# The same 2,542 operations of two linear and two windowed attention layers, issued after another table of orders, engines and PSUM banks

## The chip, the cores and the metric

The kernel runs on one NeuronCore of a Trainium2 chip. The core has five instruction queues that run beside one another and meet only at semaphores: TensorE (PE, the matrix engine, with its weight loads shown apart as PEld), ScalarE (ACT), VectorE (DVE), GpSimd (POOL) and SyncE (SP, which only issues DMAs here). The program gives each queue a written order. The metric is the device time of one execution in microseconds, less is better; the time before is 410.37 us, the median of three runs (410.02 to 410.41).

## The reference

The input is x, 2048 tokens by 512 features, in bf16. Four layers are added to it one after the other, A, B, A, B, with shared weights for the two A and for the two B:

```python
x = x + A(layernorm(x));  x = x + B(layernorm(x));  x = x + A(layernorm(x));  x = x + B(layernorm(x))
# A: linear attention, 32 heads of 16
pq, pk = phi(q), phi(k)                # phi(t) = (t + 1 if t > 0 else exp(t)) + 1e-6
kv = sum over tokens of pk^T v;  z = sum of pk
o = (pq @ kv) / (pq . z + 1e-6);  out = o @ wo
# B: attention in a causal window of 256 tokens, 32 heads of 16
p = softmax(q k^T / 4, masked);  out = (p @ v) @ wo
```

## The kernel before, in words

The 2048 tokens are 16 tiles of 128, numbered 0 to 15. A class `Plan` writes down every piece of work as an `Op` in a dependency graph; a `Kernel` replays it on the five queues. In what follows, an operation is called by its name in the plan and its tile.

The work comes in four stages that flow into one another. In the first (`layer_a_keys`), each tile is loaded into `xres` and normalised (`norm`): `stats`, `aggr` and `xn` on VectorE, `eps` on GpSimd or VectorE, `pow` on GpSimd. The normalised tile is then transposed (`transpose`, L377 and L383): tiles 0 to 4 by TensorE (`T`, then the copy `Te`), tiles 5 to 15 by a DMA that SP issues. After it follow the keys (`k`, two matmul groups, L406), the first half of the sum over tokens (`g`, L481, two groups for each tile) and the queries (`q`, two groups, L420). Keys and queries each pass through `E` (the exponential, ScalarE, L429), `E1` (VectorE, L430) and `phi` (VectorE, L431). When all 16 tiles are through, `z`, `ge`, `gv` (L495), `den`, `rec`, `spread`, `M` and `pqd` close the sum over all tokens. `fill` (L268) are ten matmuls on zeros whose result nobody reads; besides them TensorE runs nine such at its start (L984).

The second and the fourth stage (`middle`) are the B layers. For each tile: the output and residual of the A layer before (`aout`, `res`), `norm` and transpose, the projections `bq`, `bk`, `bv`, the DMAs `kd` and `vd` that SP issues to lay out keys and values, the scores `s` (L638, L677, L680), their exponentials `ex` (ScalarE, L648, L690), the masks `mk` (VectorE) and `mf` (GpSimd or VectorE, L708 and L709), the weighted sums `pv` (L729), `rcp`, `div`, the transpose `oT` and the output `bout` with its residual `res`. In the second stage the norm, keys and values of the next A layer (`k`, `v`) are worked in as tiles become ready; the third stage (`barrier(2)`) then closes that sum as before. In the last tile `b_last` splits the transpose in two halves (L764) and the output into three groups of matmuls (L775).

SP's queue begins with the loads of `setup`. Their names: `x0`, `x1`, `x2`, `x4`, `x6`, `x8`, `x12` are pieces of x (131 KB for each tile), `wAk`, `wAq`, `wAv`, `wAo`, `wBv`, `wBo` are 0.52 MB each and `wBn` is 1.05 MB. A load from `x8` on also waits for the landing of the load four places before it in this list: x0, wAk, x1, x2, wAq, x4, x6, x8, x12, wAv, wAo, wBn, wBv, wBo. So `wAo` waits for `x6`, `wBn` for `x8`, and `wBv` for `x12`.

What sets the order is not the code but `TABLE`, a compressed string of bytes. `place` unpacks it: first the place of each of the 2,542 operations in one list, then the engine of each, then the PSUM bank of each of the 1,007 tiles in PSUM. Each engine runs its operations in the order of that list. A tile that takes a bank waits for the users of the tile that had it. `place` adds one more rule, which stays as it is: a GpSimd operation that is not in `SHORT` waits for the last VectorE operation in the list before it whose name is in `WIDE` (`E1`, `xn`, `mk`, `mf`):

```python
if o.eng == "POOL" and o.name not in SHORT and wide and wide not in o.deps:
    o.deps.append(wide)
if o.eng == "DVE" and o.name in WIDE:
    wide = o
```

`synchronise` turns the dependencies into semaphore waits.

Of the kernel before, what the change touches and what calls it, by code (L numbers as in the profile page):

```python
# [11 lines left out]
P = 128  # L12
D = 512
DH = 16
S = 2048
T = 16
# [207 lines left out]
class Plan:  # L224
# [632 lines left out]


TABLE = (
    r"c-qZa1K1|VvaT*P*0yciwr$(CZQHhO+qTW@CcDXcb7%hV<eVfoo0F4!@AKUGhSk+o?^{*fGyMUCh3765goc+c9E6835CI|rLPAiG2oggihztY|-3#}`C",  # L860
    r"4r=n43a|>hzijl3kWoa6p#`avO+fK1uY;ujD@Ez2SkS$&>LDpE9e8oAQe1v8a6_D$N)JZ7i0tjaUd=@c<fq38+hjCLu%LreIXx=gZ!`=YC|392gRX3jE",
    r"8s-6Ba;xXbbJY!USjp?I9C9aCKn-420Zp80tY9=m1@zK6Hc3&>dnyIY<i)AUHIJK`<CP!bC^_O<)o%ghj9zmcUi$1Y4j7Y=t3k1dhTn*aop79W;b4Py#",
    r"x`WOxo!U?>cOGEf$#LQi-BFJUPxgXItmuE7^L4%guZOoQoA9lpZPumWzvN{Fjw!EBfV!=XHU2d|(4Y=<4N6L!H|m;p0kHSC5}a023~lW+<^DHU4HgD@(",
    r"-N}%?_Ew~MLpedY&Gw>S1syz@+B~;(TS-1;7z#BLZ;Z=H72~d$@RTG*)26YbZ!F?D3BViO&1yK*+Eo4-gR3epF{Rlrn1Qk(5QUz5ZRaj+KSyU3G)k84K",
    r"s>rH{DypKWf=~#mKvb1fy@O;bxpFGH8VzHhw#urqsbVU-%Aty@5~`$%rgEyvkW!^kxl}1tTIE({RaI3@l~Gkx0jQ($KwhY;>Zt~*vZ}6XsFtdgYOQLjT",
    r"B^QU18ZR&6ow*D6xyhUs;z3I8mo4yiE6K!tBTN6HB&9rde{Ip-~#M}{cr#}sDm(CjZq=s5j=*uYM!bFW7Rk{QjJm<VVxSU)~iEM5+<mLYQDMzlhgur85",
    r"XJ|s-xPVp1@O>tlq;1n4)H=nQE3=q&BL>YKfYvrm5+wlez+%)Mm9`9aRU^QuPcvt1fDeI;OU$t?Hm!sk*9<uu9c})vBB7u0FvswOj?m;J8A~R=3n~6#|",
    r"2);OdSl1t-)=bxQS6Au$wQRoB#QbzN;!C9ouZhSMs9I;;+<N9wUEh1*p~6-t%H&=>}HsGaJGx~ZaL42+4-)C<*9mBF&OOYK(A)jf4zmBTZtmkNt})LB&",
    r";o~m=|fm)+3sEg{nTB~AX0!)Mn@uez{XYirAq-tU<ysK`gI2aG(Vr@K&=WrCB#|wB7M`IEkgYj{nN`|RaYV}UNS0B_H^-;Z5KdPTpQcR8^AsnVr;V}Y^",
    r"#c?<uBVt;W0uy5etcaDcGVWE8FeRo_bulug!i*RN>){oZ2`{S&I1w9Q6|9Q&F*9bt)OZPF;bp9Y)$o&QhAnV5&cV6Z96zf`_(gqHKP$jS*ch{7Hq4GW@",  # L870
    r"Gf4#?^Hv)hxf4wHpN#;AtK>xH5q?UQ*bJ_!mHQ@b7E_}hS#y2`d;-`jOA5Zte`5YN-7Q3z+9LXJ7X8@iVH9uw#0>)8@pk5%z$|?FXlr*jZrZ_7QjUq4H",
    r"u(9i%YNv&PRvKuqRH#7-}h|$CxUX>V*YyIZnqJ7+b|rE3go*!mYRsx8n|6iG5UGRUOyhIxLL+)Bx2RS7U!w1jEr<T#rSu7>1_^R2(BxB#KP)@EJbG7kC",
    r"4A;x62cd+-N*gEz4<RiU?d3m@SVe29;+5B9~ExEG^PRLY~OQa_AFc~yTLfcaE@)ebx0U7CdhaS%Sm0_q;M$4)pHhv1JGpAt|)x=#buAoU%-#u?NRXJR#",
    r"~PBo||?Zf@}3OC?Jyn_dDCVj%sIEyyn_qYXXQ40EkUvW0gp`Q^bB`HEmMX4zX#iH1hjN;Hx9ENGAHXX#Il$?g+2poy&XfAEW=oEuuQhjPb4=@8A!ozq3",
    r"(^5{#MYpjbJ)lhVkXlkkBFas9s1+rmN0gqJgftz+%(Rl)QXLwsT2mWpPl@RmKBgzMidIuQ>Oeo?dwhrSs4mr`yp)gf(+4a-9jOU5rB2kD3X-9&)Sa5qa",
    r"Xf(^@g#Pm=G2eYQGc38mK+76`LuxI(kVQR184&Ur$RK4TF`nbOkHRb^`IgYf{Icx8bpI>Ej^_nw3&v|7Ro|dX)6_{5>%2F(jr<+*=PxEqwTbmcF;1~NF",
    r"gZ{4N)W1P?eoRQy3~mKhPT*uHMoxwTpIB4%$PBI58*Tq@0Y`P-!YdWhpF`qsCO8l5+~~NiV4vrQ~NcjC#{|G@M4zNE$_r=oRgw*R-Gd&~y5p4$~2OL8I",
    r"v?9is#EiN4Sp9z$bkFYTnYypEgmJNiuTX&il}7Tl5#Q7S%8<LLyQq!08n0r&M@8mH(qt>?^~g@2-~oSJ{6kJO4=a~md3!)aNVIRuB~P@IF?a!wA-nhz3",
    r"kE<QtN=^UM>c07S5QXUS&VR;fwrYV$;^Ko7d$KkmM=jIEvfs1i|UQX$`D6gOl{3HLw@3=h|;6i+nE>UsL#+RuqZ{$rJfy;4cF3%OXAQ$G%+?Ts>f9}9t",
# [189 lines left out]
```

## Time and profile before

| | |
|---|---|
| runs (median of three) | 410.37 us |
| profiled execution, first to last instruction | 408.2 us |
| what lies around the span (the median less the span) | 2.2 us |
| TensorE busy | 396.0 us, 97% |
| VectorE busy | 347.9 us, 85% |
| ScalarE busy | 344.4 us, 84% |
| GpSimd busy | 113.8 us, 28% |
| granted TensorE clock | 1.000 |

The profiled execution has no time of its own apart from its span; the 2.2 us is the part of a run that lies before the first and after the last instruction. "Busy" is the time in which at least one instruction of the engine was under way. A matmul's end is modelled and matmuls overlap, so that a busy TensorE may still wait now and then. A row of a timeline has the start, the length, the engine, the line, the operation, what is written and read, the shape, and how many instructions were merged; an idle time before it stands in brackets with what ended it. A "q" behind an engine's name is its issuing queue.

### The profile page before, as it was taken

The numbers are of one execution on the slowest core, as the hardware profiler recorded it, in microseconds if no ns is written. First come the engines' busy times: TensorE is split into PE (matmuls) and PEld (weight loads), VectorE is DVE, ScalarE is ACT, GpSimd is POOL, SyncE is SP. The second block draws the span as 40 slices with busy tenths as digits, with TensorE's granted clock in tenths as the row PEclk, the third lists the DMA queues.
The fourth block names the chain that finished last, engine by engine and source line by source line (L and its number), as shares of the span: only waits on it lengthen the run. The fifth ranks groups of instructions, "written<-read, shape, count | busy, mean of one in ns | idle before, by whom it ended". The sixth has DMA issues, their size and how long they took to land.

```text
span 408.2 us, 18082 instructions
## 1 busy us (share of the span) xinstructions
PE 396.0 (97%) x7997; PEld 263.4 (65%) x7997; DVE 347.9 (85%) x808; ACT 344.4 (84%) x443; POOL 113.8 (28%) x194
## 2 busy tenths in 40 slices
PE   8999999999999999999999999999999999999996
PEld 3654676666575566666666777676757766576664
DVE  5998799999998999888977789988898778876685
ACT  3655579999999999999998355999998999999992
POOL 3553632112253343330503202122123201302212
PEclk9999999999999999999999999999999999999999
DMA  8754014923242934344231100364225542442543
GB/s 247 243 118 104 2 42 121 184 56 97 65 119 52 132 73 108 75 104 106 62 69 36 29 2 28 89 127 78 71 76 130 143 83 61 66 121 62 118 109 104
DMA packets 67654, 37.88 MB, mean 93 GB/s; under 512 B 48248, under 2 KB 62712, under 8 KB 67576
## 3 DMA queue, kind: packets, MB, share of 16 engines
q1 hardware_dynamic: 67184, 35.67, 38.1%
q8 instruction: 63, 1.03, 1.1%
q0 software_dynamic: 384, 1.05, 0.8%
q14 instruction: 15, 0.12, 0.1%
q10 hardware_dynamic: 8, 0.00, 0.0%
HBM read 6.29 MB, written 2.10 MB: 21 GB/s over the span
## 4 chain that ended last, share of the span: by engine, by line
PE 81%; ACT 10%; DVE 7%; DMA 1%; issue 1%; DVEq 0%
PE ps L406 27%; PE ps L420 20%; PE ps L729 15%; PE ps L638 8%; ACT pb L648 7%; PE ps L680 2%; PE ps L481 2%; ACT pb L690 1%; DVE XQ L563 1%; PE ps L677 1%; DMA XQ<-vp 1%; PE ps L984 1%; PE ps L457 1%; PE ps L543 1%; PE ps L268 1%
## 5 line engine op out<-in xcount | busy, mean ns | idle before, releaser
L648 ACT ACTIVATE pb<-ps 128x1024 bf16<-128x1024 f32 (+3 forms) x224 | 198.2, 966 | 7.4 <-PE ps L638 6.2
L729 PEld LDWEIGHTS ps<-vB,pb 128*128 128x128 bf16 x2560 | 77.6, 96 | 11.5 <-issue 4.2
L729 PE MATMUL ps<-vB,pb 128*128 128x34 bf16 x2560 | 83.2, 177 | 0.3
L420 PE MATMUL ps<-xT,wBp 128*128 128x128 bf16 x1024 | 68.6, 219 | 0.1
L420 PEld LDWEIGHTS ps<-xT,wBp 128*128 128x128 bf16 x1024 | 58.4, 98 | 9.6 <-issue 4.0
L708 POOL TENSOR_SCALAR_AFFINE_SELECT pb<-pb 128x1024 bf16<-128x1024 bf16 x34 | 39.1, 1149 | 84.0 <-DVE pb L700 31.9
L429 ACT ACTIVATE tE<-ps 128x512 bf16<-128x512 f32 x64 | 38.1, 606 | 18.4 <-PE ps L406 12.1
L638 PE MATMUL ps<-XQ,kB 32*128 32x256 bf16 (+2 forms) x1024 | 48.7, 262 | 3.3 <-ACT pb L648 0.6
L574 DVE TENSOR_TENSOR xres<-ps,xres 128x512 bf16<-128x512 f32 x63 | 43.1, 685 | 9.6 <-PE ps L406 9.1
L690 ACT ACTIVATE pb<-ps 128x1024 bf16<-128x1024 f32 x50 | 49.0, 1048 | 1.3 <-PE ps L680 1.0
L406 PE MATMUL ps<-wA,XQ 128*128 128x512 bf16 x192 | 49.2, 380 | 0.7 <-DMA XQ<-vp 0.6
L369 POOL TENSOR_SCALAR ve<-mv 128x1 f32<-128x1 f32 x49 | 11.8, 240 | 127.9 <-DVE mv L368 126.9
L370 POOL TENSOR_TENSOR rs<-ve,negh 128x1 f32<-128x1 f32 x64 | 37.9, 592 | 32.0 <-DVE ve L369 27.5
L367 DVE BATCH_NORM_STATS2 stats<-xres 128x6 f32<-128x512 bf16 x64 | 43.8, 685 | 2.8 <-DMA xres<-in_A_x_dram 2.1
L638 PEld LDWEIGHTS ps<-XQ,kB 32*128 32x128 bf16 x1024 | 15.7, 92 | 31.4 <-ACT pb L648 8.3
L420 PE MATMUL ps<-XQ,wA 128*128 128x128 bf16 x512 | 34.4, 219 | 0.0
L406 PE MATMUL ps<-wBv,xT 128*128 128x512 bf16 x128 | 34.3, 380 | 0.0
L406 PE MATMUL ps<-M,XQ 128*128 128x512 bf16 x128 | 33.3, 380 | 0.2
L420 PEld LDWEIGHTS ps<-XQ,wA 128*128 128x128 bf16 x512 | 30.1, 98 | 5.1 <-issue 0.6
L406 PE MATMUL ps<-wBo,oT 128*128 128x512 bf16 x124 | 32.7, 380 | 0.6 <-DVE vp L431 0.4
L656 DVE TENSOR_TENSOR pb<-pb,tri 128x512 bf16<-128x512 bf16 x68 | 27.7, 419 | 3.7 <-ACT pb L648 3.1
L741 DVE TENSOR_TENSOR o<-ps,rc 128x256 bf16<-128x256 f32 x64 | 27.0, 422 | 1.7
(114 smaller groups left out, 545.9 us busy)
## 6 DMA issues: line engine op xcount, KB each, us to landing
vB<-vS SPq DMA_DIRECT2D x64, 136.0 KB, 2.6
kB<-vp SPq DMA_DIRECT2D x64, 128.0 KB, 2.2
wA<-in_A_wqkv_dram SPq DMA_DIRECT2D x3, 512.0 KB, 5.2
xres<-in_A_x_dram SPq DMA_DIRECT2D x2, 512.0 KB, 4.8
pb<-in_B_wqkv_dram SPq DMA_DIRECT2D x1, 1024.0 KB, 6.9
out_dram<-xres POOLq DMA_DIRECT2D x8, 128.0 KB, 2.5
out_dram<-xres SPq DMA_DIRECT2D x7, 128.0 KB, 2.0
xres<-in_A_x_dram SPq DMA_DIRECT2D x3, 256.0 KB, 5.3
```

The source lines that it names most:

```text
L367: self.on("DVE", "stats", lambda e: e.bn_stats(K.stats[:, t, :], K.xres[:, t, :]), key, dve(512), rd=[("xres", t)], wr=[("stats", t)])
L370: self.pow = self.on("POOL", "pow", lambda e: e.tensor_tensor(K.rs[:, t, :], K.ve[:, t, :], K.negh[:], ALU.pow), key + 0.03, (640, 690), r ...
L406: m = e.matmul(K.ps(ps), lhs(c), rhs(c), start=c == 0, stop=c == 3)
L420: m = e.matmul(K.ps(ps)[:, f * P:(f + 1) * P], w(c, f), xT(c), start=c == 0, stop=c == 3)
L429: self.on("ACT", "E", lambda e: e.activation(K.tE[:, s, :], K.ps(ps), ACT.Exp, bias=0.0), key, act(512), wr=[("tE", s)], ps=[ps])
L574: self.on("DVE", "res", lambda e: e.tensor_tensor(K.xres[:, t, :], K.ps(po), K.xres[:, t, :], ALU.add), key, dve(512), rd=[("xres", t)], w ...
L638: m = e.matmul(K.ps(ps[gq])[:, ns * i:ns * i + ns], K.kB[rows, j % 4, 2 * f + b, :, :], K.XQ[rows, f, q:q + ns], start=True, stop=True, ti ...
L648: return e.activation(out(h, ns).rearrange("p (f g) c -> p f g c", f=n), i, ACT.Exp, bias=0.0, scale=0.25)
L656: return e.tensor_tensor(x, x, K.tri[:, 0, :].unsqueeze(1).to_broadcast([P, 4 * n, 64]), ALU.mult)
L690: return e.activation(o.rearrange("p (f g) b c -> p f g b c", g=2), i, ACT.Exp, bias=0.0, scale=0.25)
L708: return e.affine_select(out=x, in_=x, compare_op=ALU.is_ge, fill=0.0, base=-2, pattern=[[0, 16], [-2, 64]], channel_multiplier=1)
L729: m = e.matmul(K.ps(ps)[:, 34 * u:34 * u + 34], K.P((b // 2) % rp)[:, f, gq % 2 * 2 + gq // 2, o:o + P], K.vB[:, (b // 2) % 4, b % 2, r, : ...
```

## The change

Only the string in `TABLE` is replaced. `place`, the operations, their dependencies, shapes and instructions are the same.

```diff
 TABLE = (
-    r"c-qZa1K1|VvaT*P*0yciwr$(CZQHhO+qTW@CcDXcb7%hV<eVfoo0F4!@AKUGhSk+o?^{*fGyMUCh3765goc+c9E6835CI|rLPAiG2oggihztY|-3#}`C",
...
+    r"c-qxj1GFW{vJGTrWVUVFwr$(CZQHhO+qP}n?jE#$)xFbi&CKh5Z{Az;*Iz%+$*OZABX{gT#i_a%;He`B1J4{nd|=R^z(5EH1qndFfrX&(#65RmAtZ!@gmBL#",
...
 )
```

Unpacked by the rule of `place`, the two tables differ as follows.

*Engines.* 72 operations change theirs:

| operations | from, to |
|---|---|
| `mf` 11 / 9 | VectorE to GpSimd / GpSimd to VectorE |
| `eps` 9 / 7 | VectorE to GpSimd / GpSimd to VectorE |
| `outp` 4 / 3 | GpSimd to SP / SP to GpSimd |
| `bqe` 3 / 2, `bve` 2 / 1, `bke` 1 / 0, `ve` 1 / 2, `ge` 1 / 1, `Te` 1 / 0, `oTe` 1 / 1, `recb` 1 / 3 | VectorE to ScalarE / ScalarE to VectorE |
| `c21` (clearing `vS`) 2, `zero` 2 / 1 | ScalarE to GpSimd / GpSimd to ScalarE |
| `wp` (reordering `wBp`) 2, `c24` (clearing `pb`) 1 | GpSimd to ScalarE |

In sum VectorE has 802 operations for 807, ScalarE 443 for 442, GpSimd 193 for 190, SP 236 for 235, and TensorE the same 868.

*Order on TensorE.* 565 of the 868 operations keep their place in the queue, and 728 keep their order among one another. 442 of the 1,007 PSUM tiles have another bank. The first stage in the two tables, from the start to the key matmuls of tile 7 (`k10` and `k11` are the two groups of tile 5, and so on):

```
before: fill fill T0 fill fill fill T1 k0 k1 k2 k3 fill fill q2 q3 T2 q0 q1 fill T3 fill k4 k5 T4 k6 q4 k7 fill
        k8 q6 q7 g0 g2 g4 q5 k9 g1 g3 g5 g7 g6 k10 k11 g8 k12 k13 q10 q11 g9 k14
after:  fill fill fill fill fill fill T0 fill fill fill T1 k0 k1 k2 k3 q0 fill q1 T2 q2 q3 T3 k4 k5 T4 k6 k7 g1 g3
        k8 k9 q4 q5 q6 g5 q7 g0 g2 g4 g6 k10 k11 g7 g9 k12 k13 q10 q11 k14
```

*SP's queue* in the first stage (`T5` to `T15` are the DMA transposes):

```
before: x0 x1 wAk x2 x4 wAq x6 x8 wAv x12 wBn T5 T6 T7 wAo T8 T9 T10 T11 T13 T12 T14 T15 wBv T17 ...
after:  x0 x1 wAk x2 x4 wAq x6 x8 wAv x12 wBn wAo wBv T5 T6 T7 T8 T9 T11 T10 T12 T13 T14 T15 T17 ...
```

*GpSimd at the end of the first stage.* Before, `wp`, three of the four `c10` (each an `affine_select` on `spread`, L328) and `c24` come when all keys are done. After, `c21`, `c10`, `c10`, `c21` and `zero` stand in the list between the `E1` of tile 13's keys and that of tile 15's.

*The end.* Before, TensorE's queue ends with `pv` (last half), the first half of the last tile's `oT`, the two `bout` of tile 14, the second half of `oT`, and the last tile's three `bout`. After, it ends with the first half of `oT`, `pv` (last half), the last tile's first `bout`, the second half of `oT`, the two `bout` of tile 14, and the last tile's other two `bout`.

More of the change, by code (lines that the diff above doesn't have):

```diff
@@ L864 @@
[L864 to L867, printed above, removed]
@@ new lines @@
+    r"TZj%ZVJ_r>agYJ#K^mwH<Dm}pgZ{7)HbF+14{>1tG=O%{5Zc26$PWdeE)0auP#g|I2UrM)ARg3*F3=S=Lp8_=ham=}hI-HuLc?X4025&lOoHLq4f4Vj7z~qP",
+    r"5p;r~@EN+pVpsx4ARjD+qc8=&z*U$ETVMvvgsrd*hQKvA2G?O3JcZ>j9ah3uI1Ye_+u;N}gOIobcEU7x4lm#(tbkc?11i8txCytQD1^e>5F0~d7(4}W@H7yH",
+    r"#a*x)&O&*(19yQ@;VXCzZy*=UhB*)y<6(R}18K1;yoGm=4mGC7aCi^G<9o=D889Oj!21vZBjN`zI1CctaL9x|fuKW+1+ftn!onB{6JjDvjFB-47QxJz1*<?*",
+    r"Yz$4HC>Fycm=tqEG02K#pe!WEWLOXi!3Zb?*)Tg6$B|GIM_>*t4LPv{mc&s|3M*knERB`17S_hXPzCE?Rjh{fusOEC>R1EoVhN}Wt6()$f|j@jT48H!j7_jU",
@@ L915 @@
+    r"2lJ;d_QM)5y$CP_2F~Z<^YXp%V93ivV3_dRO2BWImre2k0$KXgbBV<-4R2L>iS$Ss-#22<9}2+p!s%tt<K&;chXUU#^mNe#<iO((+UFAxBn(WkZ`FhMm}@_l",
+    r"-+c0qfk6|m6ipyIzeobf_{9AD1=t9TV_^P#hXWWX3G^$lyaN3SupQt51y+t9ra+6n0{9uw5SUIM*uN_L9C#8G@G8j{2QCDL%xCOZB!dK!4lIPg*m^#Cn><_J",
+    r"syVQdeI-x93x!aCFFu%0-_K-#JKocjXW7^Ch5nN7TYz2h;7|pM10(1={F`C`C12nx2T=1X$Ge;YoWnrEzTCTheUiQ~Fw1^e(D>Sj;z8m60KsB0`T",
 )
```

95 lines of the change are left out of this document (45 added, 50 removed).

## The prediction

> **What bounds the kernel now.** I read the page's busy times and its chain first, then the stretches of the stages, then the SP and TensorE timelines of the first 45 us, where the two tables differ most.
>
> ```profile
> span 408.2 us, 18082 instructions
> PE 396.0 (97%) x7997; PEld 263.4 (65%) x7997; DVE 347.9 (85%) x808; ACT 344.4 (84%) x443; POOL 113.8 (28%) x194
> GB/s 247 243 118 104 2 42 121 184 56 97 65 119 52 132 73 108 75 104 106 62 69 36 29 2 28 89 127 78 71 76 130 143 83 61 66 121 62 118 109 104
> PE 81%; ACT 10%; DVE 7%; DMA 1%; issue 1%; DVEq 0%
> ```
> ```profile
> 1.25 4.02 PE ps L984 x9
> ...
> 404.15 0.62 PE ps L775 x4
> ```
> ```profile
> 60.00:215.00 155.00, 152.93 (x3098) 99.72 (x3096) 139.76 (x326) 150.89 (x176) 46.88 (x71) 1.00 0.44 95
> ...
> 330.00:408.20 78.20, 70.43 (x1886) 47.95 (x1882) 58.42 (x133) 68.23 (x86) 14.23 (x20) 1.00 0.40 94
> ```
>
> TensorE is the bound. It is not busy for 408.2 - 396.0 = 12.2 us: 1.25 before its first matmul, 408.2 - 404.8 = 3.4 after its last, and 7.6 inside. The change leaves TensorE's operations alone, so that a reordering can win at most about those 7.6 us and whatever small waits the modelled ends hide; it can lose without such a limit. In the second stage (60 to 215 us) ScalarE is nearly as full, 150.9 of 155.0. In the last 78 us TensorE has its gaps, and ScalarE (68.2) is nearer to it than VectorE (58.4).
>
> So the question is where TensorE waits. The one row of the waits view that has TensorE's matmuls of L406 held by a DMA is this, a single time, at a transpose of the first stage that the chain shows too:
>
> ```profile
> PEld ps L406 <- DMA XQ<-vp: 1.1, 1, 1.1
> ```
> ```profile
> 30.57 4.23 DMA XQ<-vp
> ```
>
> **The change part by part.** *Engine choices.* VectorE sheds five operations, none longer than the casts below, so at most 5 x 0.73 = 3.7 us of 347.9; ScalarE takes one more, GpSimd three.
>
> ```profile
> L592 DVE CAST vp<-ps 128x512 bf16<-128x512 f32 x25 | 18.3, 730 | 4.3 <-PE ps L420 3.9 <-DMA kB<-vp 0.3
> L709 DVE TENSOR_TENSOR pb<-pb,tri 128x1024 bf16<-128x1024 bf16 x16 | 11.0, 690 | 0.1
> ```
>
> The cover is TensorE's own queue, full beside them. Where that cover fails, in the last 78 us, the two masks less are worth at most 2 x 0.69 = 1.4; where ScalarE has no room (60 to 215 us), one more cast there could cost up to 0.7. I take 0 and keep -1.4 and +0.7.
>
> *The first stage, up to k10.* The new queue puts six fills ahead of T0 where the old one had two. The early matmuls are slow:
>
> ```profile
> 5.07 1.06 PE L268 MATMUL ps<-kB 128*128 128x512 bf16 x2
> 5.92 0.63 PE L383 MATMUL ps<-ident,vp 128*128 128x128 bf16 x4
> 6.34 1.15 PE L268 MATMUL ps<-kB 128*128 128x512 bf16 x3
> ...
> 7.55 0.38 PE L406 MATMUL ps<-wA,XQ 128*128 128x512 bf16 x1
> ...
> 9.71 1.06 PE L420 MATMUL ps<-XQ,wA 128*128 128x128 bf16 x16
> ```
>
> Two fills take the queue from 5.07 to 5.92, 0.43 each. Six end at about 7.2. T0 then goes out near 7.2 instead of 5.92. In the old queue k0 follows 1.6 behind T0; some 0.4 of that is the slow pace of the early matmuls, so that I put it at 1.2 and k0 near 8.4. Four key groups later (4 x 0.43) it is 10.15, where the old queue began its first query at 9.7, two fills after its keys. That is a loss of 0.45. From there to k8 both tables have the same matmul work: the new one has g1 and g3 (0.86) for q4 (0.45) and two fills (0.43). So k8 moves from 15.0 to about 15.4, and after the two keys, four queries and five g that the new queue has before it (7 x 0.43 + 4 x 0.445 = 4.8), k10 could start at 20.25. The paces are from these rows of the chain:
>
> ```profile
> 9.88 0.89 PE ps L420 x16
> ...
> 36.31 2.16 PE ps L481 x10
> 38.47 0.38 PE ps L504 x16
> ```
>
> In the old queue k10 is the first of the merged row at 20.65, and gv begins at 44.66:
>
> ```profile
> 14.99 0.59 PE L406 MATMUL ps<-wA,XQ 128*128 128x512 bf16 x2
> ...
> 20.65 0.81 PE L406 MATMUL ps<-wA,XQ 128*128 128x512 bf16 x3
> ...
> 44.66 0.61 PE L495 MATMUL ps<-kB,wA 128*128 128x128 bf16 x8
> ```
>
> Between k10 and gv the new queue has 22 k, 25 g, 4 q and 4 z: 47 x 0.432 + 4 x 0.445 + 4 x 0.39 = 23.6 us. If T5 has landed, gv comes at 43.9, 0.8 earlier than now.
>
> *T5 behind the loads.* This is the term that decides. SP's old and new queue differ in that wAo and wBv now go out before T5.
>
> ```profile
> 9.66 0.37 SPq L283 DMA_DIRECT2D xres<-in_A_x_dram  x1
> 11.84 0.37 SPq L286 DMA_DIRECT2D pb<-in_B_wqkv_dram  x1
> 17.03 3.91 SPq L377 DMA_TRANSPOSE XQ<-vp  x3
> 20.98 0.59 SPq L286 DMA_DIRECT2D wAo<-in_A_wo_dram  x1
> 22.77 14.50 SPq L377 DMA_TRANSPOSE XQ<-vp  x8
> 37.32 0.58 SPq L290 DMA_DIRECT2D wBv<-in_B_wqkv_dram  x1
> ```
> ```profile
> pb<-in_B_wqkv_dram SPq DMA_DIRECT2D x1, 1024.0 KB, 6.9
> ...
> wAo<-in_A_wo_dram SPq DMA_DIRECT2D x1, 512.0 KB, 4.0
> ...
> xT<-xn SPq DMA_TRANSPOSE x28, 2.6
> ```
> ```profile
> 5.00:13.00 8.00, 8.00 (x69) 4.90 (x68) 6.66 (x20) 3.76 (x7) 4.13 (x10) 1.00 1.06 352
> 13.00:17.00 4.00, 4.00 (x41) 2.67 (x40) 4.00 (x12) 2.20 (x5) 3.04 (x9) 1.00 0.86 286
> ```
>
> wBn is issued at 11.84 and lands 6.9 later, at 18.7. wAo needs only x6 and follows it at once; wBv waits for x12, issued at 9.66, and goes out near 15. Both are then queued behind wBn: 2 x 0.52 MB at the 352 GB/s of the full queue are 3.0 us, so wBv lands near 21.7. The old table shows what a transpose behind a load does: T8, issued at 22.77 while wAo (20.98 + 4.0 = 25.0) was under way, took 2.9 where the median is 2.6, and landed at 25.7, 0.7 behind the load:
>
> ```profile
> DMA to landing us min/median/max: 2.9/2.9/2.9
> ```
>
> So T5 lands near 22.4 and holds k10, everything behind it on TensorE and, through `E`, ScalarE: 2.15 us after 20.25. gv comes at 22.4 + 23.6 = 46.0, 1.3 later than now. Low end: the rate sagged to 286 from 13 to 17 us because little was queued; if wAo fills that, wBv lands 0.9 earlier, and gv is 0.4 late. High end: the 5.8 MB of all 11 loads and two more at the 245 GB/s of the page's first two slices end near 24.5, T5 at 25, gv is 3.9 late. No wait at all gives -0.8. I take +1.3, by the row of T8. The old table's own stall at 34.8 goes; the 23.6 holds none, so it is in the sum. T6 and T7 follow T5 at some 0.7 each and are covered by four groups of 0.43.
>
> Here a page of the Trainium skill has a rule that speaks the other way: "DMA: Bandwidth & Descriptors", section "Queues, rings and completion order", has ring entries taken up in order, but without a barrier, so that a later one may finish first. By it T5 might land ahead of the loads, which is the first rival below; the landing of T8 after wAo here bears out only the order.
>
> *The other transposes.* I summed TensorE's work that the list puts between an `xn` and the first reader of its transpose, by the paces above. The tightest in the old table is T5 with 2.2 us, and TensorE did not wait for it. In the new one five have 1.2 to 2.1 (tile 14 and 12 of the second linear layer the tightest), against a landing after 2.6. If all five paid, it would be 1.4 + 0.95 + 0.65 + 0.55 + 0.5 = 4.0; if VectorE runs ahead of the list, as at T5, nothing. I take +0.5, nearer to the T5 row. Nothing below zero, since wider covers elsewhere hide no wait that the trace shows.
>
> *The port.* A VectorE operation was held by a GpSimd one in one clear place:
>
> ```profile
> 37.57 0.85 POOL L328 TENSOR_SCALAR_AFFINE_SELECT spread<-spread 128x512 bf16<-128x512 bf16 x1
> 37.65 0.92 DVE L430 TENSOR_SCALAR tE<-tE 128x512 bf16<-128x512 bf16 x1
> ```
> ```profile
> L430 DVE TENSOR_SCALAR tE<-tE 128x512 bf16<-128x512 bf16 x64 | 18.4, 292 | 2.4 <-ACT tE L429 2.0
> ```
>
> 0.92 for 0.29: a loss of 0.63, and it ends as the GpSimd operation does. The mean of all 64 `E1` is 292 with this one in it, so the old table pays this hardly more than once, and 0.63 is what it can win. The new one puts two `c10`, two `c21` and a `zero` between the `E1` of the last keys; three of these could be held, 1.9 in all. I take +0.2 net and keep -0.6 and +1.9.
>
> *The end.* Behind the last `pv` the chain now has the half transpose and two `bout`, then the other half:
>
> ```profile
> 402.70 0.86 PE ps L406 x4
> ```
>
> These 0.86 us of `bout` cover `rcp` and `div`. The new queue has one group of 0.43 there and the 0.86 behind, so that the second half waits up to 0.43 longer, and the copy behind it less. I take 0; ends 0 and +0.4.
>
> *Sum:* 408.2 + 1.3 + 0.5 + 0.2 = 410.2 us of span. With the 2.2 us that lie between this span and the median of 410.37: 412.4 us.
>
> **The rivals.** *T5 in time (the other side, faster).* If the transposes land before 20.25, TensorE keeps the -0.8, with the port's -0.6 and no other wait: 410.4 - 0.8 - 0.6 = 409.0. It decides where T5 lands before 21.1, 0.8 after 20.25. For it: the DMA share was only 0.86 from 13 to 17 us. Against it: T8.
>
> *Nothing to tell.* T5 lands near 21.1, and the rest cancels: 410.4. TensorE's waits are only 7.6 us in all, which speaks for small differences. A measurement of this kernel can tell about 0.2%, 0.8 us, from no change.
>
> *The port becomes the wait.* The three `E1` at the end of the first stage pay 1.9 where I have 0.2: 414.1. For it: the row of 0.92. Against it: only one such row. The Trainium skill, "SBUF — State Buffer", section "Who interferes with whom", has an exclusive lock by which the second to come blocks for the whole instruction; the two rows at 37.6 agree.
>
> *All loads at the slices' rate.* T5 at 25: 415.0. Against it: 352 GB/s.
>
> **How the numbers follow.** My forecast has 0.50, with a range of its own from 411.3 to 413.9; T5 in time 0.24; nothing to tell 0.16; the port 0.06; the slow loads 0.04. Slower is 0.50 + 0.06 + 0.04 = 0.60, the same 0.16, faster 0.24. The range from 408.8 to 414.3 reaches past the first rival's 409.0 and takes in the port's 414.1; it leaves out the slow loads and the far end of the first rival.
>
> **What would show it.** In the SP timeline, T5 issued near 15.5 and landing after wBv, above 21.5; on TensorE, an idle time for a DMA before the keys of tile 5, k10 at 22 to 23, and L495 first at 45 to 47. `E1` rows (L430) of more than 0.6 between 40 and 46 us would show the port. More waits of L406 and L420 for transposes between 60 and 250 us would show the covers. I am wrong if k10 starts by 21 or L495 by 44.7, or if the second half of the trace gains or loses more than 1.5 us against the first: there I have no term beyond the covers, the casts and masks.

## The result and the profile after

The changed kernel takes 415.39 us (median of six runs, 414.62 to 416.80), the kernel before, run beside it, 410.35. The ratio is 1.0118, with a 95% interval from 1.0092 to 1.0144: 5.0 us slower, where 2.0 were forecast. The profiled execution has a span of 413.3 us, 5.1 more than before.

The page of the changed kernel, its span, busy times, DMA rate in 40 slices and the chain that ended last:

```profile
span 413.3 us, 18007 instructions
PE 387.0 (94%) x7923; PEld 263.6 (64%) x7997; DVE 347.5 (84%) x803; ACT 345.0 (83%) x444; POOL 117.2 (28%) x197
GB/s 248 318 72 65 2 28 116 173 80 82 81 117 43 109 90 120 67 120 95 53 67 46 25 2 28 67 135 68 100 95 87 127 71 58 85 112 96 121 121 78
PE 72%; ACT 11%; DVE 8%; DMA 5%; issue 2%; POOL 1%; SPq 0%
```

74 matmul records are missing in this trace (7923 of 7997), so TensorE's busy sum is not to be compared; its weight loads are complete, and the times below are those of first weight loads. The chain says what is new: DMAs carry 5% of it, where it was 1%.

Where the 5.1 us arise, from the start of the same operations in both traces:

| | before | after | later by |
|---|---|---|---|
| `T` of tile 0 / `k0` | 5.49 / 7.50 | 7.24 / 8.33 | 1.75 / 0.83 |
| `k10` (first reader of T5) | 20.43 | 22.74 | 2.31 |
| `gv` (L495) | 44.63 | 46.94 | 2.31 |
| `bq` 31 in the second stage | 189.70 | 191.82 | 2.12 |
| `den` 4, close of the second sum | 241.19 | 244.22 | 3.04 |
| `aout` 32, start of the last layer | 244.70 | 247.45 | 2.75 |
| `bk` 40 (first reader of T52) | 269.23 | 273.32 | 4.09 |
| last `bout` | 404.27 | 408.68 | 4.40 |
| end of the span | 408.2 | 413.3 | 5.1 |

Less than half of the loss arises in the first stage. Four places can be seen. First T5, in the view of TensorE's waits (total, times, longest; the second row belongs to the fourth place), on SP, among the DMAs issued from 11 to 16.1 us (the last column is the time from issue to landing), in the chain and on TensorE:

```profile
PE ps L406 <- DMA XQ<-vp: 2.4, 1, 2.4
PE ps L420 <- DMA xT<-xn: 1.0, 1, 1.0
```
```profile
12.91 0.37 SPq L286 DMA_DIRECT2D pb<-in_B_wqkv_dram  x1
13.32 0.51 SPq L286 DMA_DIRECT2D wAo<-in_A_wo_dram  x1
15.71 0.37 SPq L290 DMA_DIRECT2D wBv<-in_B_wqkv_dram  x1
16.12 7.17 SPq L377 DMA_TRANSPOSE XQ<-vp  x4
```
```profile
pb<-in_B_wqkv_dram SPq DMA_DIRECT2D x1, 1024.0 KB, 6.4
wAo<-in_A_wo_dram SPq DMA_DIRECT2D x1, 512.0 KB, 7.5
wBv<-in_B_wqkv_dram SPq DMA_DIRECT2D x1, 512.0 KB, 6.5
```
```profile
16.12 6.58 DMA XQ<-vp
```
```profile
22.74 1.04 PE L406 MATMUL ps<-wA,XQ 128*128 128x512 bf16 x4 [2.38 <-DMA XQ<-vp]
```

The loads land at 19.3, 20.8 and 22.2; T5, by the chain's piece, at 16.12 + 6.58 = 22.70, and TensorE starts 0.04 later.

Second, GpSimd at the end of the first stage, in the merged timeline of VectorE, GpSimd and TensorE:

```profile
41.41 1.02 POOL L340 MEMSET vS<- 128x1106 bf16 x1
41.77 0.81 DVE L430 TENSOR_SCALAR tE<-tE 128x512 bf16<-128x512 bf16 x1 [0.28 <-ACT tE L429]
...
42.91 1.90 POOL L328 TENSOR_SCALAR_AFFINE_SELECT spread<-spread 128x512 bf16<-128x512 bf16 x2
43.23 0.87 DVE L430 TENSOR_SCALAR tE<-tE 128x512 bf16<-128x512 bf16 x2
...
44.89 0.61 PE L481 MATMUL ps<-vp 128*128 128x512 bf16 x2 [0.36 <-DVE vp L431]
```

Two `E1` of 0.29 take 0.81 and 0.68 (0.87 for the pair in which the first is held); the last `g` wait for the `phi` behind them. From `k10` to `gv` the changed kernel takes 24.20 us. Four kernels below with the same order on TensorE up to there and these GpSimd operations moved back (b1, b2, b3, e4) take 23.67 to 23.78, so that their place costs 0.4 to 0.5 us.

Third, and forecast by no term, the same at 200 us: an `xn` on VectorE and a mask `mf` 23, which the change moved to GpSimd, and the `pv` that waits for the masks `mk` behind that `xn`:

```profile
199.69 1.32 DVE L371 TENSOR_SCALAR xn<-xres,mv,rs 128x512 bf16<-128x512 bf16 x1
```
```profile
199.72 1.15 POOL L708 TENSOR_SCALAR_AFFINE_SELECT pb<-pb 128x1024 bf16<-128x1024 bf16 x1 [0.45 <-ACT pb L690]
```
```profile
201.73 1.37 PE L729 MATMUL ps<-vB,pb 128*128 128x34 bf16 x48 [0.55 <-DVE pb L656]
```

The group of all 48 such `xn` has a mean of 441 ns (21.1 us) where it was 404 (19.4); two of them, here and at 140.6 us, make the whole difference. The groups of before and, below it, after:

```profile
L371 DVE TENSOR_SCALAR xn<-xres,mv,rs 128x512 bf16<-128x512 bf16 x48 | 19.4, 404 | 1.1 <-POOL rs L370 0.7 <-DMA XQ<-xn 0.2
```
```profile
L371 DVE TENSOR_SCALAR xn<-xres,mv,rs 128x512 bf16<-128x512 bf16 x48 | 21.1, 441 | 0.8 <-POOL rs L370 0.8
```

Fourth, T52 in the last layer, on SP and TensorE:

```profile
267.54 1.20 SPq L619 DMA_DIRECT2D vB<-vS  x2
268.78 0.61 SPq L600 DMA_DIRECT2D kB<-vp  x1
269.44 2.63 SPq L377 DMA_TRANSPOSE xT<-xn  x1
```
```profile
273.33 0.84 PE L420 MATMUL ps<-xT,wBp 128*128 128x128 bf16 x12 [0.98 <-DMA xT<-xn]
```

T52's `xn` was ready at 268.16. The transpose is issued 1.3 us later, since SP issues two `vd` and a `kd` first, and lands at 273.28, 3.84 after its issue and 0.56 behind the landing of that `kd`. Before, T52 stood ahead of the two `vd`: it was issued 0.25 behind its `xn`, took 4.16, and TensorE did not wait for it.

### The profile page after: what moved, and what is told of

Its sections match the earlier page's. It is cut to its first block, busy times and chain, and to the rows that moved or that the text cites. A ratio compares the mean times of both kernels' runs of the same rounds, so it can differ in the third digit from the quotient of the medians.

```text
span 413.3 us, 18007 instructions
## 1 busy us (share of the span) xinstructions
PE 387.0 (94%) x7923; PEld 263.6 (64%) x7997; DVE 347.5 (84%) x803; ACT 345.0 (83%) x444; POOL 117.2 (28%) x197
## 3 DMA queue, kind: packets, MB, share of 16 engines
q8 instruction: 63, 1.03, 1.1%
## 4 chain that ended last, share of the span: by engine, by line
PE 72%; ACT 11%; DVE 8%; DMA 5%; issue 2%; POOL 1%; SPq 0%
PE ps L406 23%; PE ps L420 18%; PE ps L729 15%; ACT pb L648 8%; PE ps L638 7%; PE ps L481 2%; PE ps L680 2%; DMA XQ<-vp 2%; DMA XQ<-xn 1%; DMA xT<-xn 1%; PE ps L457 1%; PE ps L543 1%; ACT pb L690 1%; DVE vp L431 1%; DVE stats L367 1%
## 5 line engine op out<-in xcount | busy, mean ns | idle before, releaser
L708 POOL TENSOR_SCALAR_AFFINE_SELECT pb<-pb 128x1024 bf16<-128x1024 bf16 x36 | 42.0, 1166 | 72.1 <-DVE pb L700 35.6
L406 PE MATMUL ps<-wA,XQ 128*128 128x512 bf16 x181 | 46.7, 380 | 4.1 <-DMA XQ<-vp 2.4
L406 PE MATMUL ps<-wBv,xT 128*128 128x512 bf16 x110 | 30.7, 380 | 2.2 <-issue 1.3
L740 DVE RECIPROCAL rc<-ps 128x16 f32<-128x16 f32 x64 | 16.2, 253 | 18.3 <-PE ps L729 17.9
L406 PEld LDWEIGHTS ps<-wA,XQ 128*128 128x128 bf16 x192 | 16.5, 98 | 23.0 <-DMA XQ<-vp 2.9
L406 PE MATMUL ps<-M,XQ 128*128 128x512 bf16 x113 | 29.7, 380 | 1.3 <-issue 0.8
L406 PE MATMUL ps<-wBo,oT 128*128 128x512 bf16 x100 | 27.5, 379 | 3.3 <-issue 1.8
```

Of the source, the lines that this page charges most:

```text
L406: m = e.matmul(K.ps(ps), lhs(c), rhs(c), start=c == 0, stop=c == 3)
L708: return e.affine_select(out=x, in_=x, compare_op=ALU.is_ge, fill=0.0, base=-2, pattern=[[0, 16], [-2, 64]], channel_multiplier=1)
L740: self.on("DVE", "rcp", lambda e: e.reciprocal(K.rc[:, s, h, :].rearrange("p (u a) -> p u a", a=2), v()[:, :, :, 16]), key + 0.02, dve(16, ...
```

## The experiments

Fifteen kernels ran, e2 twice; each time below is a median, with the ratio to the kernel before on the same chip (its median 410.1 to 410.7). The operations are the same in all, only order, engines and banks differ, and c1 and c2 add matmuls that nobody reads. "Early" and "late" at a place are against the profile of before, as in the table above.

**The first stage of one table, the rest of the other.** The seam is at the first `den`.

```diff
 h1: +new order and banks up to den 0 |  old order behind it   (wBv at its old place, behind T15)
 h2:  old order up to den 0           | +new order behind it
```

> The first stage (up to den of the first token group) in the new order, with the new engines and banks, and everything behind it as before. Theory: the first stage's loss of 2.3 us (gv at 46.9 for 44.6) is carried to the end unchanged, since TensorE has few waits behind it that could take it up: 412.7 us, 0.5% to 0.7% slower than before. Rival: the loss is taken up by waits later, and the change loses its 5 us in the later stages: 410.4 to 411.0.

412.85 us, 1.0053 [1.0020, 1.0085]. This is not the test that it was meant to be: of the two loads only `wAo` goes ahead of T5, `wBv` keeps its old place behind T15. In the profiled execution (410.06 us) `wAo` landed at 20.1 and T5 at 20.6, and `k10` was only 0.2 late, so that the 2.3 us never arose. The median lies 2.8 above this execution. 5 of the 12 runs have a mean clock of 0.996 or less (414.6 on average, the other seven 411.5); where it fell is not on record. What the profile does show is that a delay of 0.4 us behind the first sum stays within 0.1 up to 332 us: the old rest neither gives back nor adds.

> The counterpart: the first stage as before, everything behind den of the first token group in the new order. Theory: 415.4 - 2.3 = 413.1 us, so that the later stages hold the larger half of the loss, some 2.7 us. Rival (the later losses only come from a first stage that ends late, by other meetings of transfers): close to 410.4. Rival (the first stage's loss is taken up later anyway): 415.

414.95 us, 1.0106 [1.0072, 1.0140]. Not a clean test: at the seam TensorE waits 2.05 us for `recb`, which stands behind four `wp` on ScalarE. The two views of h2:

```profile
49.05 0.40 PE L556 MATMUL ps<-rec,spread 32*128 32x128 bf16 x16 [2.05 <-ACT rec L548]
```
```profile
46.24 2.59 ACT L355 ACTIVATE wBp<-pb 128x512 bf16<-128x512 bf16 x4
48.71 0.28 ACT L548 ACTIVATE rec<-recf 128x128 bf16<-128x128 f32 x1
```

But from the first `aout` (+2.0) to the last `bout` (+3.9) it loses 1.9, as the changed kernel does (+2.3 to +4.4 is 2.1). So the later loss belongs to the later order.

**The loads alone.**

```diff
 e1 (new table):  SP: ... wBn
-wAo wBv T5 T6 T7 T8 ... T15
+T5 T6 T7 wAo T8 ... T15 wBv
 e2 (old table):  SP: ... wBn
-T5 T6 T7 wAo T8 ... T15 wBv
+wAo wBv T5 T6 T7 T8 ... T15
 e5 (old table): as e2, with wBv left at the end
```

> The new table with two entries of SP's queue moved back: wAo behind the transpose of tile 7, wBv behind that of tile 15. Theory (the transposes wait for the loads ahead of them): T5 lands 2.5 us after its issue, near 18.7, k10 starts near 20.4 and not at 22.7, and the time falls by 1.8 to 2.3 us, to about 413.3. Rival (VectorE, full in this stage, is the second bound and the stage would have been late anyway): k10 early, but gv still after 46 and the time within 0.6 of 415.4.

412.6 us, 1.0047 [1.0022, 1.0072]. `k10` is 0.5 early, `gv` 0.3 early, the last `bout` 2.5 late. By the medians, from 1.0118 to 1.0047, the place of two loads is worth some 2.9 of the 5.0 us; by the two profiles 2.6 at `gv` and 2.0 at the last `bout`. The rest, 1.9 by the medians, is lost behind the first stage.

> The old table with only wAo and wBv moved ahead of the transpose of tile 5. Theory: T5 lands 0.5 behind wBv, near 22, k10 starts near 22.5 in place of 20.4, and the time rises by 1.2 (if the old wait before tile 12 goes with it) to 2.2 us: 411.6 to 412.6. Rival: the old order has other work to fill the gap, under 0.4 us lost: 410.4 to 410.8.

413.42 us, 1.0063 [1.0035, 1.0090], more than expected. The profile has a second price behind the wait: TensorE's timeline, and a row of stretches whose columns are the stretch and the busy times of PE, PEld, DVE, ACT, POOL, the granted clock, the DMA share and GB/s:

```profile
22.52 1.74 PE L406 MATMUL ps<-wA,XQ 128*128 128x512 bf16 x4 [2.38 <-DMA XQ<-vp]
```
```profile
22.70:26.10 3.40, 3.40 (x9) 1.21 (x8) 1.07 (x3) 0.60 (x1) 0.00 (x0) 0.50 0.53 43
26.10:30.00 3.90, 3.90 (x31) 2.27 (x30) 2.71 (x8) 2.81 (x5) 1.59 (x4) 1.00 0.17 34
```

For 3.4 us behind the wait the clock is granted at one half, and four keys take 1.74 us where they take 1.04. `k10` is 2.1 late and everything from tile 12 on 3.9.

> The old table with wAo alone (0.52 MB) ahead of T5; wBv stays at the end of the loads. With both, T5 landed near 22 us. Theory 'the queue lands in order': T5 lands one load earlier, 1.5 us, near 20.8, and k10 is at most 0.5 late: 410.9, with no fall of the clock. Rival 'any load ahead of T5 costs the whole': T5 lands near 22 with one load as with two, 412.4 to 413.4.

410.69 us, 1.0021 [1.0000, 1.0043]. The landings, each from the issue and the DMA view:

| kernel | last load ahead of T5, landing | T5 landing | `k10` |
|---|---|---|---|
| before | wBn 18.7 | 19.5 | 20.43 |
| e5 | wAo 20.4 | 21.0 | 21.03 |
| e2 | wBv 22.0 | 22.5 | 22.51 |
| e2 again, another chip | wBv 21.1 | 21.6 | 21.61 |
| after | wBv 22.2 | 22.7 | 22.74 |

T5 lands 0.5 to 0.8 behind the load ahead of it, whichever that is. In the first row T5 took 2.5 us from its issue at 17.03, the time of most transposes with nothing ahead of them, so that this row does not show the load holding it; the other four do. The Trainium skill, "DMA: Bandwidth & Descriptors", section "Queues, rings and completion order", allows a later entry to finish first; no transpose in these rows did.

**Zeros in place of the wait.** e2 with one `fill` before `k10`, made of six (c1) or twelve (c2) matmuls on zeros that nobody reads.

```diff
 e2: ... g5 g7 g6
+fill (6 or 12 matmuls)
 k10 k11 ...
```

> The old table with wAo and wBv ahead of T5, as in the earlier run (413.4, where T5 landed near 22 us, TensorE waited 2.4 us before k10, and the granted clock fell to half for 3.4 us behind it), but one fill moved to just before k10 and made of six matmuls, about 2.5 us, so that TensorE works on zeros while T5 is awaited; no other work is changed. Theory 'the idle time halves the clock': k10 stays near 22.4, but the stretch behind it runs at full clock, the loss is the wait's 2.0 alone, 412.4, and the mean clock is 0.998 or more in nearly all runs (0.996 or less in 8 of the 12 of the earlier kernel). Rival 'chance': the clock falls in as many runs as before, 413.4.

413.3 us, 1.0062 [1.0037, 1.0086]. The six take 1.46 us, not 2.5, and leave a wait of 1.50. `k10` and tile 8 are both 2.4 to 2.5 late: no half clock behind the wait.

> Once more the old table with wAo and wBv ahead of T5, beside the next kernel on one chip. The earlier run: 413.4, mean clock 0.996 or less in 8 of 12 runs, T5 at 22.5. Theory 'the idle time halves the clock': again more than a third of the runs at 0.996 or less, and 412.5 to 413.5. Rival 'that chip, that hour': hardly a run below 0.998, 411.5 to 412.

412.02 us, 1.0042 [1.0018, 1.0066]. Here T5 landed at 21.6, the wait was 1.13, and the clock behind it stayed whole. The mean clock of this profiled execution is 0.996 all the same: it fell in the last layer, from 388.65 to 392.06 us, behind a stop of TensorE for which the view names no other engine:

```profile
388.10 0.36 PE L638 MATMUL ps<-XQ,kB 32*128 32x224 bf16 x5 [1.29 <-issue]
```
```profile
388.65:392.06 3.41, 3.08 (x56) 1.71 (x53) 1.46 (x4) 3.19 (x4) 0.00 (x0) 0.50 0.26 60
```

So a low mean clock does not tell that it fell behind T5.

> The same with twelve matmuls on zeros (0.215 us each by the earlier run of six, 2.6 us) where TensorE would wait for T5. Theory 'the idle time halves the clock': k10 at 22.5 to 22.9 as without them, at most one run in twelve at 0.996 or less, 412 to 412.6, some 0.5 to 1 less than the kernel without. Rival 'the zeros change nothing': the same share of runs with a lower clock and the same time; the earlier run with six took 413.3, which speaks for it.

414.02 us, 1.0090 [1.0061, 1.0118], slower than without the zeros on the same chip. TensorE is busy up to 22.97:

```profile
20.38 2.75 PE L268 MATMUL ps<-kB 128*128 128x512 bf16 x12
22.97 1.03 PE L406 MATMUL ps<-wA,XQ 128*128 128x512 bf16 x4
```

T5 had landed at 22.0, so the zeros themselves held `k10`; of the 2.0 us beside e2 again that is some 0.8, and the rest is open (this profile loses another 1.5 between 134 and 159 us, where e2 again loses none). What is left is a count: a mean clock of 0.996 or less (3.4 us at one half make 0.996) in 8 of 12 runs of e2, 3 of 12 of e2 again, 1 of 6 and 1 of 10 with zeros, and 6 of 126 of the kernel before. The counts differ, but they do not say where the clock fell; a fall right behind the wait for T5 is shown by one profile alone, that of e2. Filling the wait with zeros is no cure.

**One stage of the new order alone.**

```diff
 s2:  old up to aout 17 (102 us) | +new up to q 46 (243 us) |  old
 s4:  old up to q 46 (243 us)    | +new
```

> The new table for the second stage and the close of its sum alone (from the output of tile 1 of the first window layer, near 102 us, to the close of the second sum, near 243 us); all before and behind it by the old table. In the changed kernel's trace this stretch loses 1.0 us, from +2.05 to +3.04. Theory 'held VectorE': GpSimd's masks hold an xn (0.4 us becomes 1.3) near 139 and near 198 us, the second of them makes the masks of pv 48 late, and TensorE waits 0.5 to 0.8 there: 411.4, two xn rows above 1.2 us, and the loss at pv 48. Rival 'phase': the stretch loses only because the late first stage shifted what meets what (loads, DMAs, engines); begun on time it costs nothing: 410.4, and no idle time before pv 48.

412.01 us, 1.0025 [1.0003, 1.0046]. Begun on time, the stretch still loses 1.4 us (+0.3 at `aout` 17, +1.74 at `den` 4), 0.8 of it at `pv` 48 as above:

```profile
198.59 1.32 DVE L371 TENSOR_SCALAR xn<-xres,mv,rs 128x512 bf16<-128x512 bf16 x1
```
```profile
200.63 0.54 PE L729 MATMUL ps<-vB,pb 128*128 128x34 bf16 x15 [0.55 <-DVE pb L656]
```

The `xn` at 139 us was not held here, against the expectation; which operation a mask meets there turns on small shifts. Of the 3.1 us that this profile is late at its end, 0.4 arise at the seam behind `den` 4 and 1.0 in the old order of the last layer, with a stop as in e2 again.

> The old table to the close of the second sum (near 243 us), the new one for the last window layer. The changed kernel's trace loses 1.4 us there: 1.1 before bk 40 of tile 4 (a transpose issued behind three other DMAs of SP) and 0.3 at the end. Theory 'queue': the loss comes whole with the order, 411.8, with an idle time of about 1 us before the keys of that tile that a DMA ends. Rival 'long transposes by chance': a transpose's 3.8 us is a matter of what it meets and not of this order: 410.4 to 410.8, no such idle time.

412.70 us, 1.0035 [1.0009, 1.0062]. Before `bk` 40 TensorE waits again, and this time the transpose is issued at 267.59 and lands at 271.39, 0.46 behind the `kd` ahead of it:

```profile
271.43 0.73 PE L420 MATMUL ps<-xT,wBp 128*128 128x128 bf16 x10 [0.94 <-DVE mv L368]
```

(The view names VectorE, whose `mv` was long done; the landing at 271.39 is what precedes.) From `aout` 32 to `bk` 40 it loses 1.3, as in the changed kernel. Another 0.45 arise at its seam.

**Cures, one upon the other.**

```diff
 e3 = e1 and
-POOL: c21 c22 c10 c10 c21 zero between the E1 of the last keys
+POOL: the same behind the last phi
-mf 23, mf 11 on GpSimd
+mf 23, mf 11 on VectorE, behind mk 49 and xn 30
-SP: vd35 vd34 kd37 T52
+SP: T52 vd35 vd34 kd37
```

> The changed table with wAo and wBv behind T7 and T15 as in the earlier run (412.6), and three more edits: c21, c22, c10, c10, c21, zero behind the E1 and phi of the first stage's last keys; the masks mf 11 and mf 23 on VectorE behind the xn that they held; the transpose T 52 ahead of vd 35, vd 34 and kd 37 in SP's queue. Theory 'held VectorE and queue': 0.7 back before L495 near 44 us, 0.9 back at pv 48, 1.0 at bk 40: 412.6 - 2.6 = 410.0. Rival 'the masks cost VectorE as much as they free': an mf on VectorE is 0.69 us of a full queue, and the DMAs that T 52 passes are late in its place: only the 0.7 comes back, 411.9.

412.6 us, 1.0048 [1.0027, 1.0070]: in sum nothing. Place by place, `gv` is 1.05 early, 0.77 more than in e1. Of that 0.38 is there at `k10` already, so that the GpSimd edit is worth 0.4 here; `pv` 48 waits no longer, `bk` 40 neither, its start 0.5 later against `aout` 32 and not 1.7. T52 is now issued 0.02 behind its `xn`; it still takes 3.46, with nothing before it in SP's queue under way, so that the earlier issue is what helped. But the close of the first sum takes 1.6 back: `spread` needs the last `c10`, which now runs 1.6 us later than in e1:

```profile
47.60 0.41 PE L556 MATMUL ps<-rec,spread 32*128 32x128 bf16 x16 [1.54 <-POOL spread L328]
```
```profile
46.60 0.85 POOL L328 TENSOR_SCALAR_AFFINE_SELECT spread<-spread 128x512 bf16<-128x512 bf16 x1
```

And `mf` 11 on VectorE helped nothing: another mask held the same `xn` instead.

> The changed table with its loads put back, c21 to zero behind the last E1 and mf 11 on VectorE, up to pv 36 (near 163 us); the old table from there on. In the earlier run the new order so far stood at -0.54 us; with 0.7 from the GpSimd edit it would be -1.2: 409.2, the first version faster than the one before. Rival: TensorE has its work to do and what is won at the start is lost where ScalarE is full (150.9 of 155.0 us busy from 60 to 215 us): 409.9 to 410.4.

410.3 us, 0.9985 [0.9961, 1.0009]. b1 is e3's start with the old table from `pv` 36 on. It has the same wait for `spread` and is 0.15 late at the end.

> As the version before (the changed table's start, loads put back), but of the GpSimd operations moved behind the last E1 the three c10, which the first spread needs, come first; the old table from pv 25 on (near 131 us). Before, spread waited for the third c10 until 47.3 and the output of the first A layer began 0.45 late; it could begin 1.2 earlier, as the sum was 1.15 early at L495. Theory 'the wait only moved': the output begins near 49.3, TensorE is 0.7 to 1.0 early at 131 us and stays so: 409.5. Rival 'given back where ScalarE is full': early by 0.7 at 50 us, and by less than 0.2 at 131 us: 410.2.

410.81 us, 1.0008 [0.9989, 1.0026]. With the three `c10` first, `aout` begins 1.0 early and `pv` 24 is 1.7 early, the most of any run. Then the seam costs it all: TensorE waits 1.5 us at 131.8 for the exponentials of the old order, and the end is 0.3 early. 8 of its 12 runs have a mean clock of 0.996 or less (411.1 on average, the other four 410.0), so that its median lies above its profiled execution, 409.65.

> The changed table with loads put back, the GpSimd operations behind the last E1 with the three c10 first, mf 23 on VectorE behind mk 49, T 52 ahead of vd 35 in SP's queue, and the old table from pv 91 on (near 332 us). Against the earlier cured run (412.6): 1.2 less in the close of the first sum, 0.3 less where mf 11 stays on GpSimd, 0.5 less at the end: 410.6. What is left of the changed order are its waits before k 48 and k 60 and what it wins from 60 to 180 us. Rival: the waits follow one another, and what is cured in one place is waited for in the next, as with spread: 411.6 or more.

409.88 us, 0.9991 [0.9968, 1.0014]. e4 keeps the new order up to `pv` 91 with the loads back, the `c10` first, `mf` 23 on VectorE and T52 ahead, and takes the old table behind it. No wait for `spread`, at `pv` 48 or at `bk` 40 is left, and the last `bout` is 0.1 early: with these edits the 5 us are gone.

> The cured order (409.9) with two more cures, the old table from the close of the second sum on (den 4, near 241 us): T 36 ahead of kd 27 in SP's queue (it landed 0.6 behind that transfer, 4.2 us after its issue, and TensorE waited 0.6 before k 48), and the residual of tile 15 ahead of a phi on VectorE (TensorE waited 0.6 before k 60 for its bank). The cured order stood at -0.46 at den 4. Theory 'each wait adds': -1.0 to -1.6 there and to the end: 409.0 before the scatter of 0.3. Rival 'TensorE catches up in the close of the sum whatever came before': -0.5, 409.8.

409.37 us, 0.9973 [0.9950, 0.9995], the one version whose interval lies below the kernel before, by 0.05 to 0.5%. Its profiled execution does not show why: wBn landed at 20.8 in it, T5 at 21.3, and it ends 0.6 late. T36 ahead of `kd` 27 and the residual ahead of the `phi` took away the waits before `k48` and `k60`, but counted from `gv`, `den` 4 comes no earlier than in e4 (0.2 gained in both). So those two waits were given back, and its step over e4 (409.88) is within the scatter.

> The same two cures, but the cured new order kept to q 62 (near 294 us) with T 52 ahead of vd 35, the old table from there on. It stood at -0.44 at that point. Theory 'each wait adds': as the version before within 0.3, 409.1. Rival: the last layer's start of the changed order loses 0.3 however T 52 is placed, 409.8.

410.08 us, 0.9988 [0.9963, 1.0013]; not to be told from e4 or from before.

## Why the prediction was wrong in size

The way was right, the mechanism of the largest term too. What failed is the rest: the sum had 0.5 us behind `gv`, and 2.8 were measured there. The terms behind it were mis-sized or put at nothing: the other transposes (+0.5), the engine choices (0) and the end (0). Up to `gv` it had 1.5, and 2.3 were measured.

*The first stage up to k10* held as a sum, and in part by luck. By the matmul rows T0 was put at 7.2 (7.25), k0 at 8.4 (8.35), k8 at 15.4 (15.39). But T0 was put there for six slow fills, and these were through at 6.63. T0 then waited for the `xn` of tile 0, which ended at 7.19 and before at 5.27, because the new order of VectorE has the statistics of tile 1 ahead of it:

```profile
7.25 0.40 PE L383 MATMUL ps<-ident,vp 128*128 128x128 bf16 x4 [0.62 <-DVE vp L371]
```

From `k10` to `gv` the sum had 23.6 without a wait; b1, b2, b3 and e4 took 23.67 to 23.78. "No wait at all gives -0.8" for `gv`: -1.04 to -1.15 in e3, b1 and b2, where neither T5 nor the port holds it.

*T5 behind the loads* held: T5 near 22.4 (22.70), `k10` behind it. The sum then had `gv` at 46.0; its matmul row came at 46.96, of which 0.3 is T5 and 0.4 to 0.5 the port. One price was missing, a lower clock. Of the changed kernel's six runs three have a mean clock of 0.996 or less, and their mean is 416.2, that of the others 414.8. By these it is some 0.7 of the 5.0, an estimate from six runs; where the clock fell in them is not on record. The changed kernel's own profile has it whole behind a wait of 2.38 us, as long as that of e2:

```profile
22.50:26.10 3.60, 3.36 (x26) 1.95 (x27) 1.34 (x4) 1.15 (x2) 0.79 (x2) 1.00 0.71 72
```

The wait of 2.05 in h2 was followed by no fall either. So the length of a wait alone does not decide it. The Trainium skill's "TensorE: Matmul & The Clock Gate", Part 1, puts the fall of the clock after at least one idle window of about 3.4 us. The falls here last 3.41 us, but the 3.41 us ahead of them were not idle: TensorE was busy for 1.03 of them in e2 and for 2.12 in e2 again. The measurement decides: less than a whole idle window was enough.

*The port* at +0.2 was too small by 0.2 to 0.3 at `gv`: two `E1` were held, not three, and they cost 0.4 to 0.5; the range had this, the chosen value took them as bought off by the 0.63 of before. The larger error is that it was looked for in one place alone. Of the engine choices I asked what VectorE sheds (0.69 for each `mf`), not whom the mask would hold on GpSimd: `mf` 23 costs 0.9 on an `xn` and 0.8 on TensorE at `pv` 48. s2 repeats it, and e3, with the mask on VectorE, has no wait there.

*The other transposes* at +0.5 failed by their rule. I set each cover against one landing time, 2.6 us from an `xn` that SP takes up at once. T52, the costliest, loses 1.3, and that is SP's own queue: the transpose goes out 1.3 behind its `xn` in the changed kernel, e1, h2 and s4, and 0.02 to 0.03 behind it in e3 and e4, where TensorE waits no longer. The transfer took 3.3 to 4.2 us in all of these and before, whatever stood ahead of it; why it takes more than 2.6 is open. Tile 8 of the second linear layer (`k48`) waited 0.7 for T36, which landed 0.6 behind a `kd`. Tile 14 of that layer, one of the tightest in the sum, waited too, 0.5 on TensorE's weight loads, but for a bank: `k60` started 0.05 behind a residual's end at 234.75, and T46 had landed at 234.17.

*The end* at 0 was 0.1 on TensorE, within its range: the kernel is 4.33 late at 398 us, ahead of the last `pv`, and 4.40 at the last `bout`. From there to the end of the span it loses 0.7 more, which I had not costed. 0.2 of that lies before the last output's DMA is issued (the residual of tile 14, moved late with its `bout`, stands on VectorE ahead of the last two). The other 0.5 is that DMA itself: it takes 2.04 us from issue to landing for 1.56. The other late outputs now go out close ahead of it, GpSimd's last and that of tile 14 both 0.85 earlier, where they went 2.7 and 1.4 earlier. It is no accident: from the last `bout` to the end take 4.55 to 4.62 us in all five profiles with the new end, 3.96 or 3.97 in the twelve with the old one. That the outputs slow one another was not tested apart.

In all, by the table: +2.3 to `gv`, -0.2 to 190 us, +0.9 to the close of the second sum, -0.3, +1.3 at T52, +0.3 from there to the last `bout` and +0.7 behind it, 5.1 with the rounding. The sentence that I would be wrong if the second half lost more than 1.5 us named the right place: behind `gv` it lost 2.8.

Of the rivals, "T5 in time" fell with T5 at 22.7. "The port becomes the wait" was right in its mechanism, in two places, with 0.4 to 0.5 at `gv` and 0.8 at `pv` 48 on TensorE. The single causes are shown by undoing them (loads, GpSimd's place, `mf` 23, T52); the end is shown by the kernels that have it and those that do not; the clock's share is only counted.

## What to carry to other kernels

Cost a transpose by what stands ahead of it in its queue, wherever it stands: it goes out only when SP has issued the DMAs before it (1.3 us for T52), and behind a load it lands about 0.5 us after it. When work is given to GpSimd, ask which VectorE operation will run beside it and who waits for that one; the time saved on VectorE is not the price. Count the outputs too: those that were moved close ahead of the last one cost 0.7 us behind the last matmul. And before a queue's operations are moved behind a stage, look up who needs the last of them: the cure of one wait (0.4 in e3) made another of 1.5 until the needed ones came first.

## What the runs showed that was not expected

- TensorE's clock fell to 0.50 for 3.4 us behind a wait of 2.38 us in e2, and behind a stop of 1.29 us at 388 us in e2 again. In 17 profiles no other fall stands before the last matmul. The mean clock was low in 11 of 24 runs of that kernel against 6 of 126 of the kernel before. With zeros in the wait it was low in 2 of 16 runs, but the kernel was no faster. b2, which waits 1.5 us at 131.8, had it in 8 of 12 runs; s4, which waits 0.7 at 243 and 0.9 at 271, in none of 12. What decides is open.
- Between 384 and 391 us TensorE stops inside one operation, a group of matmuls that no semaphore interrupts: 0.54 us on its weight loads before, 0.71 after, 1.46 in e2 again, and not over 0.3 in six of the 17 profiles. The profiles of h1 and e5 win 0.2 to 0.4 there against before, those of s2 and e2 again lose 0.6 and 1.8. Why it stops is not shown.
- On SP no transpose overtakes: of 1,408 in the 17 profiles none landed ahead of a transfer issued before it. Where such a transfer landed more than 1.9 us after the transpose's issue, the transpose followed within 0.8 us in 319 of 371 cases, 0.6 in the median. Of 315 with nothing ahead of them under way most took about 2.5 us, but 84 took 3.0 to 4.7; why is open.
- The same load lands at quite different times: wBn at 17.3 (e2 again), 18.7 (before), 19.3 (after) and 20.8 (b3), issued between 11.6 and 12.9 in all of them. In b3 T5 came 0.5 behind it, at 21.3, and TensorE waited 1.64 for it, with both later loads back at their old places. The old order has wBn ahead of T5 as well; whether it waits in some executions is not shown.
- A wait of VectorE for GpSimd goes to the end of the GpSimd operation, by the records 0.15 beyond it: 1.32 for an `xn` of 0.40, beside a mask of 1.15 that began 0.03 behind it.
